# Gated linear attention and two MoE layers on one core: attention rebuilt around VectorE block transposes, alternating row halves, block-diagonal states and merged scans

## The chip, the core and the metric

The kernel runs on one core of a Trainium2 chip. The metric is the device time of one execution in microseconds, taken as the median of several runs. TensorE (PE) multiplies matrices, VectorE (DVE), ScalarE (ACT) and GpSimd (POOL) work on elements, SyncE (SP) issues most of the transfers. Each engine takes its instructions in the order in which the program lists them and waits on semaphores for the others.

## What is computed

Three steps follow one another: a gated linear attention over 4 batches, 8 heads, 768 tokens and a head width of 48, a gated MoE layer, and a mixture of four domain experts.

```python
for t in range(S):                      # attention, per batch and head
    state = alpha[:, :, t, :, None] * state + np.einsum('bhd,bhe->bhde', k[:, :, t], v[:, :, t])
    y[:, :, t] = np.einsum('bhd,bhde->bhe', q[:, :, t], state)
...
gate = 1.0 / (1.0 + np.exp(-(x @ w_gate)))        # x: 3072 x 384, d_ff 1536
x = gate * (x @ w_val) @ w_out
...
p = domain_probs / (domain_probs.sum(-1, keepdims=True) + 1e-09)
for e in range(E):                                # 4 experts of width 1024
    out += p[:, e:e + 1] * (np.maximum(x @ w1[e], 0.0) @ w2[e])
```

## The kernel before

The tokens of the attention are cut into 24 chunks of 128 (NCH; six of them, CPB, make a batch). Each chunk holds 8 heads, kept as 4 pairs (NP): one head of a pair on partitions 0 to 63 and one on 64 to 127, each 48 wide with 16 columns of padding. A chunk goes through three stages.

- Stage 1 brings alpha, k and q of a chunk, loaded token by token, into the layout with the head's width on the partitions: `s1_pe` calls `s1_t` for each, four TensorE transposes against the identity (L188), into banks 7, 6 and 5. On VectorE `s1_b` runs four scans (L203) backwards over the chunk's decays and gets the decay from each token to the chunk's end, with three small operations (L205 to L207) for the whole chunk's; `s1_k` multiplies k with it. `s1_a` runs four scans forwards (L217) for the inverse, `s1_q` multiplies q with that. `s1_range` lets ScalarE sum both for a range check, and `st_decay` decays the running state.
- Stage 2, `s2_pe`, transposes the scaled k (L233) and computes the scores, eight products of 64 rows: the four pairs of the lower half, then the four of the upper. `s2_ev` copies the transposed k out on ScalarE (L241) and masks the scores on VectorE (L244) into `pt`.
- Stage 3, `s3_pe`, multiplies transposed k with v for the state's increment, v with the masked scores, and, except in the first chunk of a batch, the old state with q. The two products for a pair of heads stand together in the order:

```python
for j in (0, 1):
    mm(X0[64 * j:64 * j + 64, p, :], vn[i][:, 2 * p + j, :], pt[j][:, p, :], True, first)
for j in (0, 1):
    r = slice(64 * j, 64 * j + 64)
    if not first:
        mm(X0[64 * j:64 * j + D, p, :], St[r, p, :], qt[i][r, p, :], False, True)
```

`s3_y` copies the result out and moves the fourth pair's part into the padding of the other three by six small transfers (L268), `s3_state` adds the increment to the state, and `s4`, two steps later, splits the result into a high and a low part as the input `xs` of the first MoE.

All fp32 products of the attention show as two matmul records each in the trace. The MoE products are three fp32r products of 512 or 384 columns each (`mm3`, all on L112).

The order of every engine is the program's own (the whole body stands under a manual schedule). A prologue takes chunks 0 to 4 through the three stages, overlapped by one chunk. The first MoE follows in six blocks of 512 tokens (bi), each in 12 steps (f). A step computes gate and value products (`gv`, 18 matmuls on banks 0 and 1), the sigmoid on ScalarE (L339), the product on VectorE (L343), its high part on ScalarE (L344) and its low part (`g_lo`: GpSimd in the first block, VectorE, L349, later), and the output products of the step before (`l2`, 9 matmuls). Into each step one stage of one chunk is woven: chunk 5 takes the first three steps, chunk 8 ends the first block, chunks 9 to 23 lie in the later ones. In the first block each step also decodes two to four units of weights that come as float64 bits: three VectorE operations a unit (L161 to L163), two on ScalarE (L155, L174), one on GpSimd, and up to four transfers on SP (L140 to L147) into four landing buffers that are refilled as they come free. Of alpha, k, q and v two chunks are held; `load` brings the next but one as soon as the transposes of a chunk have read their buffer. The second MoE follows, and takes more than half of the time; the change does not touch it.

Of the kernel before, what the change touches and what calls it, by code (L numbers as in the profile page):

```python
# [15 lines left out]
P = 128  # L16
# the scaled form holds while a chunk's running decays and their inverses stay below BOUND
# [5 lines left out]
def kernel(ctx: ExitStack, tc: tile.TileContext, q, k, v, alpha,  # L23
# [27 lines left out]
    RR = const.tile([P, 35840], F32R, tag="RR", name="RR")  # L51
    FA = const.tile([P, 9216], F32, tag="FA", name="FA")
# [3 lines left out]
    low = const.tile([P, 1], F32, tag="low", name="low")  # L56
    St = const.tile([P, NP, D], F32, tag="St", name="St")
    aend = const.tile([P, NCH * NP], F32, tag="aend", name="aend")
    pn = const.tile([P, NTT, E], F32, tag="pn", name="pn")
    psm = const.tile([P, NTT], F32, tag="psm", name="psm")  # L60
    fl = const.tile([P, (NP + 2) * NCH], F32, tag="fl", name="fl")
# [15 lines left out]
    # phase A, attention  # L77
# [21 lines left out]
    sg = [carve(LD, LT + (2 + i) * TB, TB) for i in (0, 1)]  # L99
    stg = [carve(LD, i * TB, TB) for i in range(4)]  # L100
    # phase B
# [18 lines left out]
    def load(g, part, eng=nc.sync):  # L120
        if g >= NCH:
            return
        b, c = divmod(g, CPB)
        i = g % 2
        for t, x in (((vn, v),) if part else ((an, alpha), (kn, k), (qn, q))):
            eng.dma_start(out=t[i][:, :, 0:D],
                          in_=x[b, :, c * P:(c + 1) * P, :].rearrange("h p d -> p h d"))

    # weights of MoE1 come as float64 bits: word 0 low, word 1 high
# [60 lines left out]
    def s1_pe(g, bk):  # L190
        for X, t in ((bk[2], an), (bk[1], kn), (bk[0], qn)):
            s1_t(g, X, t)
        load(g + 2, 0)

    def ends(t, g):
        return t[:, g * NP:(g + 1) * NP]

    # decay from a token to the chunk's end, and the whole chunk's
    def s1_b(g, bk):
        Bc, X0 = Ac[g % 2], pairs(bk)[2]  # L200
        lows = low.to_broadcast([P, P - 1])
        for p in range(NP):
            nc.vector.tensor_tensor_scan(Bc[:, p, 0:P - 1][:, ::-1], X0[:, p, 1:P][:, ::-1], lows, 1.0, ALU.mult, ALU.max)  # L203
        ae = ends(aend, g)
        nc.vector.tensor_tensor(ae.rearrange("p (a b) -> p a b", b=1), X0[:, :, 0:1], Bc[:, :, 0:1], ALU.mult)  # L205
        nc.vector.tensor_scalar(ae, ae, low, None, ALU.max)
        nc.vector.reciprocal(ends(fl, g), ae)  # L207

    def s1_k(g, bk):
        i = g % 2  # L210
        nc.vector.tensor_tensor(kt[i], pairs(bk)[1], Ac[i], ALU.mult)

    # its inverse, running forwards
    def s1_a(g, bk):
        X0 = pairs(bk)[2]
        for p in range(NP):
            nc.vector.tensor_tensor_scan(kb[g % 2][:, p, :], X0[:, p, :], low.to_broadcast([P, P]),  # L217
                                         ends(fl, g)[:, p:p + 1], ALU.mult, ALU.max)

    def s1_q(g, bk):  # L220
        i = g % 2
        nc.vector.tensor_tensor(qt[i], pairs(bk)[0], kb[i], ALU.mult)

    def s1_range(g, o):
        n = NP * NCH + 2 * g
        for j, t in enumerate((kb, Ac)):
            nc.scalar.activation(o, t[g % 2].rearrange("p a b -> p (a b)"), AF.Copy, accum_out=fl[:, n + j:n + j + 1])

    def s2_pe(g, bk):
        i = g % 2  # L230
        X = pairs(bk)
        for p in range(NP):
            nc.tensor.transpose(X[2][:, p, :], kt[i][:, p, :], ident)  # L233
        for j in (0, 1):
            r = slice(64 * j, 64 * j + 64)
            for p in range(NP):
                mm(X[j][:, p, :], kt[i][r, p, :], qt[i][r, p, :], True, True)

    def s2_ev(g, bk):
        X = pairs(bk)  # L240
        nc.scalar.activation(kb[g % 2], X[2], AF.Copy)  # L241
        mb = mask.rearrange("p (a t) -> p a t", a=1).to_broadcast([P, NP, P])
        for j in (0, 1):
            nc.vector.tensor_tensor(pt[j].bitcast(I32), X[j].bitcast(I32), mb, ALU.bitwise_and)  # L244

    def s3_pe(g, bk):
        i = g % 2
        first = g % CPB == 0
        X0, X1 = pairs(bk)[0:2]
        if g % CPB != CPB - 1:  # L250
            for p in range(NP):
                for j in (0, 1):
                    mm(X1[64 * j:64 * j + 64, p, 0:D], kb[i][:, p, 64 * j:64 * j + 64], vn[i][:, 2 * p + j, 0:D], True, True)
# [16 lines left out]

    def s3_state(g, bk):
        X1 = pairs(bk)[1]
        if g % CPB == 0:
            nc.vector.tensor_copy(St, X1[:, :, 0:D])
        elif g % CPB != CPB - 1:
# [465 lines left out]
```

## Time and profile before

| | |
|---|---|
| median of 3 runs | 1455.66 us (1455.57 to 1458.17) |
| span of the profiled execution | 1454.4 us |
| PE busy | 1428.7 us, 98% of the span |
| DVE busy | 686.9 us, 47% |
| ACT, POOL busy | 348.1 us, 162.9 us |
| end of the first block, from which the chain of waits is TensorE's | about 160 us |

The page is of one execution; its span lies 1.3 us below the median of the runs. A busy PE is not one at its peak, since matmuls are pipelined; what a change is worth is read from the chain of waits, stage by stage.

### The profile page before, as it was taken

How to read it: one execution, taken by the hardware profiler on the slowest of the kernel's cores; microseconds unless marked ns; L12 is line 12 of the kernel's file. 1: busy time of each engine (PE TensorE's matmuls, PEld its weight loads, DVE VectorE, ACT ScalarE, POOL GpSimd, SP SyncE). 2: the span in 40 equal slices, each digit the busy share in tenths (PEclk: the TensorE clock that was granted, in tenths of full speed). 3: DMA queues.
4: the chain of work that ended last, by engine and by line, in shares of the span. 5: the costliest groups of instructions: out<-in, count | busy, mean ns of one | idle time of the engine just before them, and what ended most of it. 6: DMA issues, size and time to landing. Idle time of an engine off the chain costs nothing.

```text
span 1454.4 us, 19314 instructions
## 1 busy us (share of the span) xinstructions
PE 1428.7 (98%) x7792; PEld 1226.1 (84%) x7792; DVE 686.9 (47%) x1235; ACT 348.1 (24%) x670; POOL 162.9 (11%) x167
## 2 busy tenths in 40 slices
PE   9889999999999999999999999999999999999998
PEld 7667787878788787879999999999999999999997
DVE  7788653434343442224444444444444444444444
ACT  3444332322222222332211111111111121111110
POOL 0344300000000000241101110110011011101000
PEclk9899999999999999999999999999999999999999
DMA  9775321312221200231000000000000000000003
GB/s 132 148 159 135 81 53 30 62 27 43 46 47 24 53 2 9 88 94 52 23 1 23 22 11 12 22 23 1 23 22 23 0 23 22 0 1 0 1 23 110
DMA packets 138640, 60.76 MB, mean 42 GB/s; under 512 B 108336, under 2 KB 133168, under 8 KB 138544
## 3 DMA queue, kind: packets, MB, share of 16 engines
q1 hardware_dynamic: 129184, 57.68, 17.1%
q10 hardware_dynamic: 9360, 1.77, 0.8%
q8 instruction: 63, 1.03, 0.3%
q14 instruction: 33, 0.27, 0.1%
HBM read 49.59 MB, written 8.65 MB: 40 GB/s over the span
## 4 chain that ended last, share of the span: by engine, by line
PE 90%; DVE 4%; DMA 3%; SPq 1%; issue 1%; ACT 0%; POOL 0%; DVEq 0%; ACTq 0%; POOLq 0%
PE bank L112 88%; PE bank L188 2%; DMA LD<-in_moe_w_gate_dram 1%; DVE LD L163 1%; DVE LD L162 1%; DMA FA<-in_q_dram 1%; DMA LD<-in_moe_w_out_dram 1%; PE bank L233 1%; SPq L268 1%; DVE LD L161 0%; DVE FA L203 0%; DVE FA L244 0%; DMA LD<-LD 0%; DVE FA L217 0%; SPq L140 0%
## 5 line engine op out<-in xcount | busy, mean ns | idle before, releaser
L112 PE MATMUL bank<-RR 128*128 128x512 f32 (+1 forms) x5976 | 1266.3, 372 | 6.4 <-ACT LD L339 2.7
L112 PEld LDWEIGHTS bank<-RR 128*128 128x128 f32 x5976 | 1092.8, 189 | 162.2 <-issue 4.2
L386 DVE SCALAR_TENSOR_TENSOR RR<-bank,RR 128x512 fp32r<-128x512 f32 x192 | 132.8, 692 | 330.9 <-ACT RR L385 330.9
L385 ACT ACTIVATE RR<-bank 128x512 fp32r<-128x512 f32 x192 | 114.9, 599 | 647.1 <-PE bank L112 647.1
L402 DVE SCALAR_TENSOR_TENSOR FA<-bank,pn,FA 128x384 f32<-128x384 f32 x360 | 221.4, 615 | 99.9 <-PE bank L112 99.9
L343 DVE TENSOR_TENSOR LD<-bank,LD 128x512 f32<-128x512 f32 x72 | 49.8, 691 | 222.4 <-PE bank L112 205.1
L369 POOL TENSOR_TENSOR RR<-LD,RR 128x384 fp32r<-128x384 f32 x64 | 63.5, 1025 | 651.3 <-PE bank L112 609.6
L112 PE MATMUL bank<-FA 64*128 64x128 f32 (+2 forms) x1088 | 95.5, 277 | 1.2 <-ACT FA L241 1.0
L112 PEld LDWEIGHTS bank<-FA 128*64 128x64 f32 (+1 forms) x1088 | 69.7, 161 | 25.0 <-issue 21.0
L339 ACT ACTIVATE LD<-bank 128x512 f32<-128x512 f32 x72 | 42.6, 592 | 174.3 <-PE bank L112 174.3
L344 ACT ACTIVATE RR<-LD 128x512 fp32r<-128x512 f32 x72 | 45.4, 631 | 140.3 <-DVE LD L343 140.3
L289 POOL TENSOR_TENSOR RR<-LD,RR 128x384 fp32r<-128x384 f32 x24 | 24.3, 1012 | 428.8 <-ACT RR L288 422.3
L203 DVE TENSOR_TENSOR_SCAN FA<-bank,low 128x127 f32<-128x127 f32 x96 | 32.5, 400 | 33.1 <-PE bank L188 33.1
L349 DVE TENSOR_TENSOR RR<-LD,RR 128x512 fp32r<-128x512 f32 x60 | 41.3, 689 | 13.4 <-ACT RR L344 13.4
L180 POOL TENSOR_TENSOR RR<-LD,RR 128x384 fp32r<-128x384 f32 x36 | 38.5, 1070 | 40.0 <-ACT RR L174 40.0
L188 PE MATMUL bank<-ident,FA 128*128 128x128 f32 x288 | 39.4, 285 | 1.7 <-ACT LD L264 1.0
L188 PEld LDWEIGHTS bank<-ident,FA 128*128 128x128 f32 x288 | 34.0, 146 | 6.3 <-ACT LD L264 1.5
L217 DVE TENSOR_TENSOR_SCAN FA<-bank,fl,low 128x128 f32<-128x128 f32 x96 | 38.4, 461 | 0.0
L163 DVE SCALAR_TENSOR_TENSOR LD<-LD 128x384 int32<-128x384 int32 x36 | 37.1, 1032 | 1.2
L244 DVE TENSOR_TENSOR FA<-bank,mask 128x512 int32<-128x512 int32 x48 | 30.9, 684 | 12.4 <-PE bank L112 12.4
L112 PE MATMUL bank<-FA,St 64*48 64x128 f32 x320 | 33.8, 288 | 0.0
L174 ACT ACTIVATE RR<-LD 128x384 fp32r<-128x384 f32 x36 | 18.8, 523 | 40.3 <-DVE LD L163 40.3
(55 smaller groups left out, 357.0 us busy)
## 6 DMA issues: line engine op xcount, KB each, us to landing
LD<-in_moe_w_dram SPq DMA_DIRECT2D x32, 384.0 KB, 3.0
FA<-in_v_dram SPq DMA_DIRECT2D x24, 192.0 KB, 2.8
LD<-in_moe_w_out_dram SPq DMA_DIRECT2D x12, 384.0 KB, 3.9
out_dram<-FA SPq DMA_DIRECT2D x24, 192.0 KB, 1.9
FA<-in_alpha_dram SPq DMA_DIRECT2D x21, 192.0 KB, 3.2
FA<-in_k_dram SPq DMA_DIRECT2D x21, 192.0 KB, 3.9
FA<-in_q_dram SPq DMA_DIRECT2D x21, 192.0 KB, 4.1
x2d<-LD SPq DMA_DIRECT2D x15, 256.0 KB, 2.3
```

Of the source, the lines that this page charges most:

```text
L112: nc.tensor.matmul(o, lhsT=l, rhs=r, start=start, stop=stop)
L163: nc.vector.scalar_tensor_tensor(wi, lw, 29, wi, ALU.logical_shift_right, ALU.bitwise_or)
L180: nc.gpsimd.tensor_tensor(unit(u, 1), wft[u % 3], unit(u, 0).bitcast(F32), ALU.subtract)
L188: nc.tensor.transpose(X[:, p * P:(p + 1) * P], t[g % 2][:, 2 * p:2 * p + 2, :].rearrange("p a b -> p (a b)"), ident)
L339: nc.scalar.activation(sg[f % 2], bank[0], AF.Sigmoid)
L343: nc.vector.tensor_tensor(s, bank[1], s, ALU.mult)
L344: nc.scalar.activation(gs[f % 2][0], s, AF.Copy)
L349: eng.tensor_tensor(gl, sg[f % 2], gh.bitcast(F32), ALU.subtract)
L369: nc.gpsimd.tensor_tensor(lo, l[:, cs], h.bitcast(F32), ALU.subtract)
L385: nc.scalar.activation(h, bk, AF.Relu)
L386: nc.vector.scalar_tensor_tensor(l, bk, 0.0, h.bitcast(F32), ALU.max, ALU.subtract)
L402: nc.vector.scalar_tensor_tensor(acc[:, tt, :], bk, pn[:, tt, e:e + 1], acc[:, tt, :], ALU.mult, ALU.add)
```

## The change

- Chunks 0 to 8 (`g < NPE`) keep the TensorE transposes, but ScalarE copies the transposed alpha into an SBUF row `Ar` before the scan reads it (`s1_al`).
- From chunk 9 on `load` brings alpha, k and q by 12 transfers of 32 partitions, four consecutive tokens to a piece, every piece into two quadrants with an offset of 32 columns; a 32x32 block transpose on VectorE (`tr32`) then takes the place of each tensor's four TensorE transposes. These chunks are loaded one chunk ahead, in one set of buffers.
- The four scans of a direction become one over 4 x 129 columns, with a column in front of each pair that resets it (`s1_b`, `s1_a`); the small operations become a memset and a reciprocal. `Bc` and `Iv` have one buffer instead of two.
- The scores alternate between the halves, on 48 rows instead of 64.
- The state `St` becomes a block-diagonal 128 x 128 matrix per pair. Its product with q comes first in stage 3, with all 128 rows and 64 columns. `s3_state` and `st_decay` work on each half apart.
- The load of the next chunks moves from the start of stage 1 to its end.

```diff
+    NPE = 9
+    BL = 32
+    TQ = P // BL
+    RB = BL + NP * TQ * D
+    ab, kbl, qb = [carve(FA, RB * i, RB) for i in range(3)]
...
+        for t, x in ((ab, alpha), (kbl, k), (qb, q)):
+            for j in (0, 1):
+                for h in (0, 1):
+                    r = BL * (2 * j + h)
+                    o = BL * (1 - h)
+                    eng.dma_start(out=t[r:r + BL, o:o + NP * TQ * D].rearrange("t (a e) -> t a e", a=NP),
+                                  in_=x[b, j:H:2, ts, :].rearrange("a (t c) d -> t a (c d)", c=TQ))
+
+    def tr32(out, t):
+        nc.vector.transpose(out.rearrange("p a (t c) -> p a c t", c=TQ),
+                            t[:, BL:].rearrange("p (a d) -> p a d", d=D)[:, :, 0:BL])
...
+    def s1_al(g, bk):
+        if g < NPE:
+            s1_t(g, bk[2], an)
+            nc.scalar.activation(At, pairs(bk)[2], AF.Copy)
+        else:
+            tr32(At, ab)
...
+    def s1_b(g):
+        nc.vector.memset(Cs[:, :, 0:1], 1.0)
+        nc.vector.tensor_tensor_scan(flat(Bc)[:, ::-1], Ar[:, 1:1 + NP * PW][:, ::-1], flat(Cs), 1.0, ALU.mult, ALU.max)
+        nc.vector.reciprocal(Cs[:, :, 0:1], Bc[:, :, 0:1])
...
+    def s1_a(g):
+        nc.vector.tensor_tensor_scan(flat(Iv), Ar[:, 0:NP * PW], flat(Cs), 1.0, ALU.mult, ALU.max)
+
+    def s1_mul(g, t, o, w, bk):
+        if g < NPE:
+            src = pairs(bk)[0]
+        else:
+            src = o[g % 2]
+            tr32(src, t)
+        nc.vector.tensor_tensor(o[g % 2], src, w[:, :, 1:PW], ALU.mult)
...
-        for j in (0, 1):
-            r = slice(64 * j, 64 * j + 64)
-            for p in range(NP):
+        for p in range(NP):
+            for j in (0, 1):
+                r = slice(64 * j, 64 * j + D)
                 mm(X[j][:, p, :], kt[i][r, p, :], qt[i][r, p, :], True, True)
...
+        def y(p, j, l, r, start):
+            nc.tensor.matmul(X0[64 * j:64 * j + 64, p, :], lhsT=l, rhs=r, start=start and p == 0, stop=True,
+                             skip_group_check=True)
+
+        if not first:
+            for p in range(NP):
+                for j in (0, 1):
+                    y(p, j, St[:, p, 64 * j:64 * j + 64], qt[i][:, p, :], True)
...
-                mm(X0[64 * j:64 * j + 64, p, :], vn[i][:, 2 * p + j, :], pt[j][:, p, :], True, first)
-            for j in (0, 1):
-                r = slice(64 * j, 64 * j + 64)
-                if not first:
-                    mm(X0[64 * j:64 * j + D, p, :], St[r, p, :], qt[i][r, p, :], False, True)
+                y(p, j, vn[i][:, 2 * p + j, :], pt[j][:, p, :], first)
...
                 if t == 1:
-                    s1_pe(g, setA)
-                    s1_b(g, setA)
+                    s1_al(g, setA)
+                    if g < NPE:
+                        s1_t(g, tk, kn)
+                        s1_t(g, tq, qn)
+                    s1_b(g)
                     s1_k(g, setA)
...
+                    if g + 2 < NPE:
+                        load(g + 2, 0)
+                    elif g + 1 >= NPE:
+                        load(g + 1, 0)
```

How the orders move. TensorE in the second block of the first MoE, one chunk from stage 1 to the end of stage 3; banks 63 and 64 hold gate and value, 65 to 67 the output, 68 to 70 are the attention's. Before:

```order
L188 MATMUL bank_68<-ident,FA 128x128 x4
L112 MATMUL bank_63<-RR 128x512 x9
L112 MATMUL bank_64<-RR 128x512 x9
L112 MATMUL bank_65<-RR 128x512 x3
L112 MATMUL bank_66<-RR 128x512 x3
L112 MATMUL bank_67<-RR 128x512 x3
L112 MATMUL bank_63<-RR 128x512 x9
L112 MATMUL bank_64<-RR 128x512 x9
L233 MATMUL bank_70<-ident,FA 128x128 x4
L112 MATMUL bank_68<-FA 128x128 x4
L112 MATMUL bank_69<-FA 128x128 x4
```

After, the same place, from the long matmuls of the step to the scores:

```order
L124 MATMUL bank_63<-RR 128x512 x9
L124 MATMUL bank_64<-RR 128x512 x9
L262 MATMUL bank_70<-ident,FA 128x128 x4
L124 MATMUL bank_68<-FA 128x128
L124 MATMUL bank_69<-FA 128x128
L124 MATMUL bank_68<-FA 128x128
L124 MATMUL bank_69<-FA 128x128
L124 MATMUL bank_68<-FA 128x128
L124 MATMUL bank_69<-FA 128x128
L124 MATMUL bank_68<-FA 128x128
L124 MATMUL bank_69<-FA 128x128
```

The 12 transposes of stage 1 are gone from this chunk, and the scores' eight products change bank, and with it the half, at every row. Stage 3 of the same chunk, before:

```order
L112 MATMUL bank_69<-FA 64x48 x8
L112 MATMUL bank_68<-FA 64x128 x2
L112 MATMUL bank_68<-FA,St 48x128 x2
L112 MATMUL bank_68<-FA 64x128 x2
L112 MATMUL bank_68<-FA,St 48x128 x2
L112 MATMUL bank_68<-FA 64x128 x2
L112 MATMUL bank_68<-FA,St 48x128 x2
L112 MATMUL bank_68<-FA 64x128 x2
L112 MATMUL bank_68<-FA,St 48x128 x2
L112 MATMUL bank_65<-RR 128x512 x3
```

And after:

```order
L124 MATMUL bank_63<-RR 128x512 x9
L124 MATMUL bank_64<-RR 128x512 x9
L282 MATMUL bank_68<-FA,St 64x128 x8
L124 MATMUL bank_69<-FA 64x48 x8
L282 MATMUL bank_68<-FA 64x128 x8
L124 MATMUL bank_65<-RR 128x512 x3
```

The state's products no longer alternate with the others and stand ahead of them. VectorE in stage 1 of such a chunk, before (L343 is the gate's product, L349 its low part):

```order
L203 SCALAR_TENSOR_TENSOR FA<-bank_70,low 128x127 x4
L205 TENSOR_TENSOR aend<-bank_70,FA 128x4
L206 TENSOR_SCALAR aend<-aend,low 128x4
L207 RECIPROCAL fl<-aend 128x4
L211 TENSOR_TENSOR FA<-bank_69,FA 128x512
L343 TENSOR_TENSOR LD<-bank_64,LD 128x512
L217 SCALAR_TENSOR_TENSOR FA<-bank_70,fl,low 128x128 x4
L222 TENSOR_TENSOR FA<-bank_68,FA 128x512
L281 TENSOR_TENSOR St<-St,aend 128x192
L349 TENSOR_TENSOR RR<-LD,RR 128x512
```

And after (the gate's product is L385, its low part L391):

```order
L154 STREAM_TRANSPOSE FA<-FA 128x4x4x32
L231 MEMSET LD 128x4
L232 SCALAR_TENSOR_TENSOR FA<-FA,LD 128x516
L233 RECIPROCAL LD<-FA 128x4
L154 STREAM_TRANSPOSE FA<-FA 128x4x4x32
L245 TENSOR_TENSOR FA<-FA 128x512
L385 TENSOR_TENSOR LD<-bank_64,LD 128x512
L237 SCALAR_TENSOR_TENSOR FA<-FA,LD 128x516
L154 STREAM_TRANSPOSE FA<-FA 128x4x4x32
L245 TENSOR_TENSOR FA<-FA 128x512
L323 TENSOR_TENSOR St<-St,FA 48x4x48 x2
L391 TENSOR_TENSOR RR<-LD,RR 128x512
```

Two block transposes come ahead of the gate's product and one behind it; none of the rows reads a bank except the gate's. ScalarE at the start of the first block, where L183 and L202 are the decode and L381 the sigmoid, after:

```order
L183 ACTIVATE LD<-LD 128x384
L202 ACTIVATE RR<-LD 128x384
L225 ACTIVATE FA<-bank_70 128x4x128
L381 ACTIVATE LD<-bank_63 128x512
L386 ACTIVATE RR<-LD 128x512
```

The copy L225 is new; it stands behind the decode and ahead of the sigmoid.

## Rows read from the trace of the kernel before

**Rows 1.** The page, parts 1 and 2: busy time by engine; granted clock in slices.

```profile
PE 1428.7 (98%) x7792; PEld 1226.1 (84%) x7792; DVE 686.9 (47%) x1235; ACT 348.1 (24%) x670; POOL 162.9 (11%) x167
...
PEclk9899999999999999999999999999999999999999
```

**Rows 2.** Chain of waits, 150 to 260 us: start, length, what, how many.

```profile
160.45 16.29 PE bank L112 x100
...
203.67 10.24 PE bank L112 x45
...
214.35 13.62 PE bank L112 x100
227.98 1.31 PE bank L188 x12
```

**Rows 3.** Timeline of TensorE, 365.5 to 377 us: start, length, engine, line, what.

```profile
365.65 1.71 PE L112 MATMUL bank<-FA 64*128 64x128 f32 x16
367.29 6.42 PE L112 MATMUL bank<-RR 128*128 128x512 f32 x27
373.63 0.91 PE L112 MATMUL bank<-FA 128*64 128x48 f32 x20
374.47 0.42 PE L112 MATMUL bank<-FA,St 64*48 64x128 f32 x4
374.82 0.44 PE L112 MATMUL bank<-FA 128*64 128x128 f32 x4
...
376.99 0.50 PE L112 MATMUL bank<-RR 128*128 128x512 f32 x1
```

**Rows 4.** Timeline of TensorE, third stages that end and begin a batch.

```profile
247.89 0.44 PE L112 MATMUL bank<-FA 128*64 128x128 f32 x4
...
250.77 2.35 PE L112 MATMUL bank<-RR 128*128 128x512 f32 x9
...
273.03 1.56 PE L112 MATMUL bank<-FA 128*64 128x48 f32 x32
274.52 2.34 PE L112 MATMUL bank<-RR 128*128 128x512 f32 x9
```

**Rows 5.** TensorE in equal windows: length, busy (instructions), clock, DMA share, GB/s.

```profile
365.75:366.19 0.44, 0.44 (x4) 1.00 0.00 0
366.19:366.63 0.44, 0.44 (x9) 1.00 0.00 0
```

**Rows 6.** Groups by line, one form each: busy us, mean ns, idle before.

```profile
L343 DVE TENSOR_TENSOR LD<-bank,LD 128x512 f32<-128x512 f32 x72 | 49.8, 691 | 222.4 <-PE bank L112 205.1 <-ACT LD L339 17.3
...
L203 DVE TENSOR_TENSOR_SCAN FA<-bank,low 128x127 f32<-128x127 f32 x96 | 32.5, 400 | 33.1 <-PE bank L188 33.1
...
L281 DVE TENSOR_TENSOR St<-St,aend 128x192 f32<-128x192 f32 x20 | 7.0, 350 | 0.1
```

**Rows 7.** Timelines of VectorE and ScalarE around 150 us.

```profile
149.37 1.25 DVE L163 SCALAR_TENSOR_TENSOR LD<-LD 128x384 int32<-128x384 int32 x1
150.54 1.34 DVE L203 TENSOR_TENSOR_SCAN FA<-bank,low 128x127 f32<-128x127 f32 x4
...
153.05 0.68 DVE L343 TENSOR_TENSOR LD<-bank,LD 128x512 f32<-128x512 f32 x1
...
150.65 0.53 ACT L174 ACTIVATE RR<-LD 128x384 fp32r<-128x384 f32 x1 [1.17 <-DVE LD L163]
```

**Rows 8.** Timeline of the prologue, ScalarE's fourth y and its transfers.

```profile
40.73 0.58 ACT L264 ACTIVATE LD<-bank 128x512 f32<-128x512 f32 x1
...
44.15 3.68 SPq L268 DMA_DIRECT2D LD<-LD  x6
```

**Rows 9.** Timeline of SP's queue at 92 us.

```profile
92.53 2.07 SPq L126 DMA_DIRECT2D FA<-in_q_dram  x1
```

**Rows 10.** Timeline of VectorE in a first stage, 225 to 234 us.

```profile
226.02 0.68 DVE L349 TENSOR_TENSOR RR<-LD,RR 128x512 fp32r<-128x512 f32 x1
...
233.51 0.69 DVE L343 TENSOR_TENSOR LD<-bank,LD 128x512 f32<-128x512 f32 x1 [2.45 <-PE bank L112]
```

More of the change, by code (lines that the diff above doesn't have):

```diff
@@ L51 @@
     RR = const.tile([P, 35840], F32R, tag="RR", name="RR")
-    FA = const.tile([P, 9216], F32, tag="FA", name="FA")
+    FA = const.tile([P, 9240], F32, tag="FA", name="FA")
     LD = const.tile([P, 6912], F32, tag="LD", name="LD")
@@ L124, in load @@
         i = g % 2
-        for t, x in (((vn, v),) if part else ((an, alpha), (kn, k), (qn, q))):
-            eng.dma_start(out=t[i][:, :, 0:D],
-                          in_=x[b, :, c * P:(c + 1) * P, :].rearrange("h p d -> p h d"))
+        ts = slice(c * P, (c + 1) * P)
+        if part:
+            eng.dma_start(out=vn[i][:, :, 0:D], in_=v[b, :, ts, :].rearrange("h p d -> p h d"))
+            return
+        if g < NPE:
+            for t, x in ((an, alpha), (kn, k), (qn, q)):
+                eng.dma_start(out=t[i][:, :, 0:D], in_=x[b, :, ts, :].rearrange("h p d -> p h d"))
+            return
+        for t, x in ((ab, alpha), (kbl, k), (qb, q)):
[8 more added lines that the diff above has]
+                            t[:, BL:].rearrange("p (a d) -> p a d", d=D)[:, :, 0:BL])
     def load_w(u):
@@ L188, in s1_t @@
             nc.tensor.transpose(X[:, p * P:(p + 1) * P], t[g % 2][:, 2 * p:2 * p + 2, :].rearrange("p a b -> p (a b)"), ident)
[L190 to L201, printed above, removed]
-        for p in range(NP):
[L203 to L207, printed above, removed]
@@ L209, in s1_k, with flat @@
-    def s1_k(g, bk):
[L210 to L218, printed above, removed]
+    def flat(t):
+        return t.rearrange("p a b -> p (a b)")
+    def s1_al(g, bk):
[4 more added lines that the diff above has]
+            tr32(At, ab)
@@ L220, in s1_q @@
+    def s1_k(g, bk):
+        s1_mul(g, kbl, kt, Bc, bk[1:])
     def s1_q(g, bk):
-        i = g % 2
-        nc.vector.tensor_tensor(qt[i], pairs(bk)[0], kb[i], ALU.mult)
+        s1_mul(g, qb, qt, Iv, bk)
     def s1_range(g, o):
-        n = NP * NCH + 2 * g
-        for j, t in enumerate((kb, Ac)):
-            nc.scalar.activation(o, t[g % 2].rearrange("p a b -> p (a b)"), AF.Copy, accum_out=fl[:, n + j:n + j + 1])
+        for j, t in enumerate((Iv, Bc)):
+            nc.scalar.activation(o.rearrange("p (a b) -> p a b", a=NP), t[:, :, 0:P], AF.Copy,
+                                 accum_out=fl[:, 2 * g + j:2 * g + j + 1])
@@ L269, in s3_y, with diag @@
                                   in_=y[64 * j + sp * c:64 * j + sp * (c + 1), NPM, :])
+    def diag(j):
+        return St[64 * j:64 * j + D, :, 64 * j:64 * j + D]
     def s3_state(g, bk):
         X1 = pairs(bk)[1]
[L273 to L276 removed]
+        for j in (0, 1):
+            x = X1[64 * j:64 * j + D, :, 0:D]
+            if g % CPB == 0:
+                nc.vector.tensor_copy(diag(j), x)
+            elif g % CPB != CPB - 1:
+                nc.vector.tensor_tensor(diag(j), x, diag(j), ALU.add)
     def st_decay(g):
         if g % CPB:
[L280 to L281 removed]
+            for j in (0, 1):
+                ae = Bc[64 * j:64 * j + D, :, 0:1].to_broadcast([D, NP, D])
+                nc.vector.tensor_tensor(diag(j), diag(j), ae, ALU.mult)
     def s4(g):
@@ L529 @@
                 nc.gpsimd.memset(t[i][:, :, D:HW], val)
-        nc.vector.memset(low, 1.0 / BOUND)
         nc.vector.memset(one, 1.0)
-        for i in (0, 1):
-            nc.vector.memset(Ac[i][:, :, P - 1:P], 1.0)
+        nc.vector.memset(Cs, 1.0 / BOUND)
+        nc.vector.memset(Ar, 0.0)
+        nc.gpsimd.memset(St, 0.0)
         nc.scalar.activation(flt, one, AF.Sigmoid)
```

48 lines of the change are left out of this document (26 added, 22 removed).

## The prediction

> **What bounds the kernel now.** I read the page's busy line first: TensorE is busy 98% of the 1454.4 us span, VectorE 47%, and the granted clock is at its upper level (2.4 GHz) in nearly every slice [rows 1]. A busy share alone does not say that TensorE is the limit, so the second view is the chain of waits. From 160.45 us on it is a chain of TensorE pieces with nothing between them [rows 2]: per attention chunk 12 input transposes (1.31 us), 45 long matmuls (10.24 us, so 0.228 us each), 4 transposes of kt (214.35 - 203.67 - 10.24 = 0.44 us), and a piece of 13.62 us that holds the scores, the long matmuls around them and the whole third stage. In that stretch every microsecond taken off TensorE is a microsecond off the end, unless another engine comes late instead. Before 160 us it is different: VectorE decoding weights, the SP queue and DMA alternate on the chain, and TensorE savings there count for nothing. Chunk 8's second and third stage and all of chunks 9 to 23 lie behind that point. So the sum is made over 16 score stages, 16 third stages and 15 first stages; the profiled execution's span lies 1.3 us under the median of 1455.66 us, and I take the savings off the median.
>
> **Input transposes (chunks 9 to 23).** The 12 matmuls of a first stage go; VectorE transposes 32x32 blocks in their place. The chain prices them at 1.31 us per chunk [rows 2], and each was 0.109 us of TensorE time. 15 x 1.31 = 19.7 us. No reason lets this be a loss on TensorE itself.
>
> **Scores.** Eight fp32 products are 16 matmul records of 64 rows. Before, all of the lower half come first, then all of the upper; from the first of them to the next long matmul it takes 367.29 - 365.65 = 1.64 us [rows 3]. After, the halves alternate. Do two halves run at once? The windows say that they do where the queue happens to offer both: 0.44 us in the middle of the stage hold 9 records where the 0.44 us before hold 4 [rows 5]. Eight records of one half at the even pace (0.44 us for 4, 0.11 us each) and a drain of some 0.2 us is 1.09 us, if the other half hides under them. I take 1.64 - 1.09 = 0.55 us; the ends are 0 (no overlap beyond today's) and 0.82 (half of 1.64, as if nothing overlapped today). 16 x 0.55 = 8.8 us.
> By the Trainium skill ("TensorE: Matmul & The Clock Gate", Part 3, The mechanism) matmuls start and end strictly in program order; then the first half could not overlap with the second in today's order, and the change would gain the 0.82. The jump from 4 to 9 records in equal windows speaks against that, but matmul ends in a trace are modelled.
>
> **State products.** Before, in a usual chunk each pair of pt products (128 rows x 64 columns) alternates with a pair of state products (64 x 48). Each group of four records takes 374.82 - 374.47, about 0.35 us, although four records that share the array two and two would need 0.22. The whole stage runs 376.99 - 373.63 = 3.36 us [rows 3]. A chunk that starts a batch has no state products: its kb and pt products stream through in 274.52 - 273.03 = 1.49 us [rows 4]. The change gives the state products the same 128 x 64 shape and puts all eight ahead of the others, so its stage is that stream plus eight pairs at 0.11 us: 1.49 + 0.89 = 2.38. The saving is 0.98 us in 11 chunks. In the three chunks that end a batch (no kb products) it was 250.77 - 247.89 = 2.88 [rows 4]; 1.49 less eight pairs of 48 columns (0.50) plus 0.89 is 1.88, saving 1.0. Chunks 12 and 18 start batches and save nothing. 11 x 0.98 + 3 x 1.0 = 13.8 us. The ends: 0, if the drains stay, and 13.8.
>
> **VectorE in the first stage.** This is the new cover that must hold. A chunk's first stage loses eight scans and three small operations and gets three block transposes (T each), two scans of 516 columns, a memset and a reciprocal; the state's two updates become four. The trace has no transpose on VectorE. Plain operations give 350 ns for 192 columns and 691 for 512, so 1.07 ns a column on 145 ns; a scan of 127 columns in 400 ns is then 2.0 ns a column, and 516 columns are 1.18 us [rows 6]. T is bounded below by the 512-column operation, 0.69 us, and above by the scan's pace, 145 + 512 x 2.0 = 1.17 us; I take 0.7, as no arithmetic is repeated in it. By the skill's page "VectorE: DVE Perf Modes" (The three transpose paths) a 128x128 bf16 tile takes 311 ns; four of them would be an estimate of 1.24 us for T, with the same sum.
> Is there room? VectorE gets past the previous step's last operation at 226.02 + 0.68 = 226.7, 227.1 with the longer state update [rows 10], and no longer waits for transposes. kt is ready at 227.1 + 2T + 2.1 (memset, scan, reciprocal, product), the gate product follows the matmuls, and qt, decay and the gate's low part end at about 233.1 + 3T even if T pushes the gate product. The second long block that needs that low part comes 45 long matmuls, 4 transposes and the scores (10.24 + 0.44 + 1.1) after the point where the 12 transposes stood, 227.98 [rows 2]: at 239.8. So TensorE starts to wait only from T = 2.2 us; before the change VectorE stood idle 2.45 us in that place [rows 10]. I cost it at nothing.
>
> **Loads.** Each chunk from 9 on comes by 12 transfers instead of 3, in 768-byte pieces instead of 192, and each piece twice. SP issues them a step and more ahead, within a chunk of 23 us; what is queued behind them there (v, the y moves) is used two steps later. Cost nothing.
>
> **The first 160 us.** Chunks 0 to 8 keep TensorE transposes and get a ScalarE copy of alpha ahead of the scan. ScalarE works in order, so the scan now waits for what is queued before the copy. In the first block the scan followed the decode directly (149.37 + 1.25, scan at 150.54) and the gate product came at 153.05 [rows 7]. Now: the rest of the decode's ScalarE step to 151.18, copy 0.58, scan and small operations 1.5, kt 0.66: about 153.85, +0.8. The second scan gives back 0.4, the two extra state operations cost 0.7: +1.1 for four chunks, +4.4. In the prologue three copies of 0.58 with about 0.5 of queue each make the fourth y 3.2 us later; it was ready at 41.31 and its moves were issued only at 44.15 [rows 8], so 2.8 of that is covered: +0.4. Against this the loads move behind the step's weight load, and chunk 9's leave a decode step: SP spent 2.07 us on one q load [rows 9], with a weight load as the next row of its queue; twice that is -4. Sum about +1. Ends: nothing covered, 9 copies at 1.2 plus 4 x 0.7 = +13.6; or only the gain, -4.
>
> **Sum.** 19.7 + 8.8 + 13.8 = 42.3 saved, 1 lost: 1455.66 - 41.3 = 1414.4 us.
>
> **Rivals.**
> (a) The copies queue for longer than I think and nothing covers them: +13.6 instead of +1, 1427 us. For it: VectorE and SP are on the chain there. Against: DMA waits of the same stretch hide part. 13%.
> (b) Alternating halves don't overlap, because a switch between halves costs what a switch of shape costs: 1423. Against: [rows 5]. 7%.
> (c) Scores gain the full 0.82, the rule of the Trainium skill above: 16 x 0.27 less, 1410. 6%.
> (d) The state products still drain, so the change doesn't do there what it says: 1428. For it: nothing in the trace has that accumulate order. 3%.
> (e) Slower: block transposes on VectorE become the bound of a first stage. They write with a stride, and the trace has no such row. Beyond T = 2.2 each microsecond of T costs 3 us in 15 chunks; the gain of 41.3 us (2.75 a chunk) is gone at T = 2.2 + 0.92 = 3.1 us, 4.5 times the 512-column row; at T = 3.5 the time is 1414.4 + 15 x 3.9 = 1473. 5%, of which 4 beyond 3.1 us or close to it.
> The forecast itself keeps 66%.
>
> **How the numbers follow.** The forecast's own spread is about +-6 us, mostly the first 160 us (the chain's piece right behind them, [rows 2], took 16.29 us where the same piece later took 13.62). With (c) below and (a), (b), (d) above, the range is 1405 to 1428. It leaves out (e) and the tails of the others. Two kernels this long are told apart at 0.2%, 3 us: faster 0.95, same 0.01, slower 0.04.
>
> **What would show it.** The chain after 160 us should have no transpose piece of 1.31 us from chunk 9 on; scores should take about 1.1 us from first record to the next long matmul, a usual third stage 2.4. A chunk's period should fall from 25.6 to about 22.8 us, with TensorE without idle time. Block transposes should be 0.7 to 1.2 us on VectorE. The first block should end within some microseconds of 160. I am wrong if TensorE waits for VectorE in the first or second stages of chunks 9 to 23, if the scores keep 1.6 us, or if the first block ends past 170.

## The result, and the profile after

| | before | after |
|---|---|---|
| median of the runs | 1455.73 us (1455.57 to 1458.17) | 1421.07 us (1420.57 to 1421.63) |
| ratio, 95% interval | | 0.9757 [0.9743, 0.9771] |
| span of the profiled execution | 1454.4 us | 1418.9 us |

The change is faster by 34.7 us, 2.4%; the forecast was 41.3 us. The time lies inside the range and 6.7 us above the forecast. The page of after, parts 1 and 2, answers to [rows 1]:

```profile
PE 1375.0 (97%) x7612; PEld 1196.4 (84%) x7612; DVE 741.7 (52%) x1151; ACT 353.6 (25%) x679; POOL 165.8 (12%) x171
...
PEclk9898999999999999999999999999999999999999
```

TensorE has lost 180 records (15 chunks of 12 transposes) and 53.7 us of busy time, VectorE has gained 54.8 us. The chain of waits of after, 165 to 260 us (start, length, what, how many), answers to [rows 2]:

```profile
176.21 1.88 PE bank L124 x7
...
200.80 1.02 PE bank L282 x16
201.82 0.45 PE bank L124 x16
202.27 0.89 PE bank L282 x16
203.16 12.47 PE bank L124 x54
215.63 0.44 PE bank L262 x4
216.06 7.44 PE bank L124 x43
223.50 1.02 PE bank L282 x16
```

It is TensorE's alone from 176.21 us on (before from 160.45), and the piece of 12 transposes is gone. From one third stage to the next it takes 223.50 - 200.80 = 22.70 us. The timeline of TensorE in a later chunk of after, 335 to 354 us, answers to [rows 3]:

```profile
335.63 1.09 PE L282 MATMUL bank<-FA,St 128*64 128x128 f32 x16
336.55 0.62 PE L124 MATMUL bank<-FA 128*64 128x48 f32 x16
337.00 1.06 PE L282 MATMUL bank<-FA 128*64 128x128 f32 x16
337.99 12.54 PE L124 MATMUL bank<-RR 128*128 128x512 f32 x54
...
350.89 1.16 PE L124 MATMUL bank<-FA 48*128 48x128 f32 x16
351.99 2.34 PE L124 MATMUL bank<-RR 128*128 128x512 f32 x9
```

The third stage takes 337.99 - 335.63 = 2.36 us instead of 3.36, the scores 351.99 - 350.89 = 1.10 instead of 1.64. The groups by line of VectorE (busy us, mean ns, idle before) answer to [rows 6]:

```profile
L154 DVE STREAM_TRANSPOSE FA<-FA 128x512 f32<-128x512 f32 x45 | 48.7, 1083 | 0.1
L232 DVE TENSOR_TENSOR_SCAN FA<-FA,LD 128x516 f32<-128x516 f32 x24 | 31.3, 1302 | 17.8 <-ACT FA L225 17.1
L237 DVE TENSOR_TENSOR_SCAN FA<-FA,LD 128x516 f32<-128x516 f32 x24 | 29.3, 1221 | 0.0
```

A block transpose takes 1.08 us. The first scan waited 17.1 us in all for the copy L225 on ScalarE, all of it in chunks 0 to 8. That VectorE is still no bound later is seen in its timeline at the gate product of such a chunk's first stage, where it idles until TensorE delivers, as in [rows 10]:

```profile
344.51 0.69 DVE L385 TENSOR_TENSOR LD<-bank,LD 128x512 f32<-128x512 f32 x1 [1.52 <-PE bank L124]
```

The gain does not begin at 160 us. Here is the first record behind chunk 8's third stage, on TensorE's timeline, of before:

```profile
174.37 2.37 PE L112 MATMUL bank<-RR 128*128 128x512 f32 x9
```

and of after:

```profile
180.38 2.79 PE L124 MATMUL bank<-RR 128*128 128x512 f32 x11
```

After is 6.0 us late at this point. From here to the end before takes 1454.4 - 174.37 = 1280.0 us and after 1418.9 - 180.38 = 1238.5: 41.5 us saved.

### The profile page after: what moved, and what is told of

The parts are those of the page before. It is cut to its first block, busy times and chain, and to the rows that moved or that the text cites. A ratio compares the mean times of both kernels' runs of the same rounds, so it can differ in the third digit from the quotient of the medians.

```text
span 1418.9 us, 19045 instructions
## 1 busy us (share of the span) xinstructions
PE 1375.0 (97%) x7612; PEld 1196.4 (84%) x7612; DVE 741.7 (52%) x1151; ACT 353.6 (25%) x679; POOL 165.8 (12%) x171
## 3 DMA queue, kind: packets, MB, share of 16 engines
q10 hardware_dynamic: 9360, 1.77, 0.9%
## 4 chain that ended last, share of the span: by engine, by line
PE 87%; DVE 6%; DMA 3%; ACT 1%; issue 1%; SPq 1%; POOL 0%; DVEq 0%; ACTq 0%; POOLq 0%
PE bank L124 84%; PE bank L282 2%; DVE LD L191 1%; DVE LD L190 1%; DVE LD L189 1%; DVE FA L232 1%; DVE FA L273 1%; DMA LD<-in_moe_w_gate_dram 1%; DMA LD<-in_moe_w_out_dram 1%; DMA LD<-LD 1%; DMA FA<-in_alpha_dram 1%; PE bank L262 1%; DMA LD<-in_moe_w_val_dram 1%; DMA FA<-in_k_dram 0%; DVE FA L237 0%
## 5 line engine op out<-in xcount | busy, mean ns | idle before, releaser
L385 DVE TENSOR_TENSOR LD<-bank,LD 128x512 f32<-128x512 f32 x72 | 49.7, 691 | 175.3 <-PE bank L124 158.7
L381 ACT ACTIVATE LD<-bank 128x512 f32<-128x512 f32 x72 | 42.8, 594 | 147.6 <-PE bank L124 147.6
L391 DVE TENSOR_TENSOR RR<-LD,RR 128x512 fp32r<-128x512 f32 x60 | 47.9, 798 | 13.4 <-ACT RR L386 12.6
L154 DVE STREAM_TRANSPOSE FA<-FA 128x512 f32<-128x512 f32 x45 | 48.7, 1083 | 0.1
L124 PE MATMUL bank<-FA 48*128 48x128 f32 (+1 forms) x704 | 42.4, 262 | 0.3 <-DVE FA L245 0.3
L124 PEld LDWEIGHTS bank<-FA 48*128 48x128 f32 (+1 forms) x704 | 36.7, 170 | 5.9 <-issue 4.9
L232 DVE TENSOR_TENSOR_SCAN FA<-FA,LD 128x516 f32<-128x516 f32 x24 | 31.3, 1302 | 17.8 <-ACT FA L225 17.1
L282 PE MATMUL bank<-FA 128*64 128x128 f32 x384 | 28.5, 282 | 6.3 <-DVE FA L273 6.2
L202 ACT ACTIVATE RR<-LD 128x384 fp32r<-128x384 f32 x36 | 18.9, 524 | 45.4 <-DVE LD L191 41.7
L237 DVE TENSOR_TENSOR_SCAN FA<-FA,LD 128x516 f32<-128x516 f32 x24 | 29.3, 1221 | 0.0
L282 PEld LDWEIGHTS bank<-FA 128*64 128x64 f32 x384 | 22.7, 141 | 7.8 <-DVE FA L273 6.5
```

The costliest lines, as they stand in the source:

```text
L124: nc.tensor.matmul(o, lhsT=l, rhs=r, start=start, stop=stop)
L154: nc.vector.transpose(out.rearrange("p a (t c) -> p a c t", c=TQ), t[:, BL:].rearrange("p (a d) -> p a d", d=D)[:, :, 0:BL])
L232: nc.vector.tensor_tensor_scan(flat(Bc)[:, ::-1], Ar[:, 1:1 + NP * PW][:, ::-1], flat(Cs), 1.0, ALU.mult, ALU.max)
L282: nc.tensor.matmul(X0[64 * j:64 * j + 64, p, :], lhsT=l, rhs=r, start=start and p == 0, stop=True, skip_group_check=True)
L385: nc.vector.tensor_tensor(s, bank[1], s, ALU.mult)
L391: eng.tensor_tensor(gl, sg[f % 2], gh.bitcast(F32), ALU.subtract)
```

## Experiments

Each edit is made in after. The kernels ran in groups, each on one chip; the difference named is to a kernel of the same group, the ratio to the kernel before on the same chip.

**Three changes undone, one at a time.** First after itself, as the measure of its group.

> The changed kernel once more, on the chip of the next three runs, as their base. Every theory expects 1421 us within 1.5 us, with a first block that ends about 9 us later than before the change and a chunk period of 22.7 us behind it.

It took 1421.85 us, ratio 0.9755 [0.9739, 0.9772].

Scores in the old order:

```diff
-        for p in range(NP):
-            for j in (0, 1):
+        for j in (0, 1):
+            for p in range(NP):
                 r = slice(64 * j, 64 * j + D)
                 mm(X[j][:, p, :], kt[i][r, p, :], qt[i][r, p, :], True, True)
```

> The changed kernel with the eight score products in the old order, the lower half's four and then the upper's. If alternating lets the two row halves run side by side, as I forecast, the score stage goes back from 1.1 to 1.64 us and 16 chunks behind the first block cost 16 x 0.55 = 8.8 us more: about 1430. If nothing overlapped in the old order, as matmuls strictly in program order would have it, it is 16 x 0.82: about 1434. If the order of the halves does not matter: 1421.

1430.72 us, ratio 0.9816 [0.9800, 0.9833]: 8.9 us slower than after. The timeline of TensorE in this kernel shows the scores and what follows them:

```profile
357.38 1.71 PE L124 MATMUL bank<-FA 48*128 48x128 f32 x16
359.01 6.20 PE L124 MATMUL bank<-RR 128*128 128x512 f32 x26
```

The stage is 1.63 us long again, although it has 48 rows as in after: the order makes the difference, not the rows. This decides rivals (b) and (c). By the Trainium skill ("TensorE: Matmul & The Clock Gate", Part 3, The mechanism) matmuls start and end strictly in program order; 16 x 0.82 = 13.1 us would then have been lost here. The measured 8.9 us does not agree with that and fits 16 x 0.55. The starts of the records in the trace of before do not agree either: the first record of the upper half starts at 366.20 us, and three of the lower half's eight start behind it, the last at 366.53, though all of them stand ahead of it in the program. So TensorE does not start its products strictly in the order in which the program lists them.

State products in the old order and shape:

```diff
-        if not first:
-            for p in range(NP):
-                for j in (0, 1):
-                    y(p, j, St[:, p, 64 * j:64 * j + 64], qt[i][:, p, :], True)
...
-                y(p, j, vn[i][:, 2 * p + j, :], pt[j][:, p, :], first)
+                mm(X0[64 * j:64 * j + 64, p, :], vn[i][:, 2 * p + j, :], pt[j][:, p, :], True, first)
+            for j in (0, 1):
+                if not first:
+                    r = slice(64 * j, 64 * j + D)
+                    mm(X0[64 * j:64 * j + D, p, :], St[r, p, 64 * j:64 * j + D], qt[i][r, p, :], False, True)
```

> The changed kernel with the state products back as 64 x 48 pieces, alternating pair by pair with the others (the block-diagonal state is kept, only its diagonal blocks are read). If each switch of shape drains the array, as I forecast, a usual third stage goes back from 2.4 to 3.35 us and 14 chunks behind the first block cost 13.8 us more: about 1435. If the saving came from the shorter wait for the masked scores alone, TensorE being busy anyway, it stays at 1421.

1440.89 us, ratio 0.9889 [0.9872, 0.9905]: 19.0 us slower, 5 more than expected. TensorE's timeline gives a third stage of 350.44 - 347.09 = 3.35 us, 0.99 more than in after, and 14 x 0.99 = 13.9 us is what was expected:

```profile
347.09 0.91 PE L124 MATMUL bank<-FA 128*64 128x48 f32 x20
...
350.44 1.89 PE L124 MATMUL bank<-RR 128*128 128x512 f32 x7
```

The rest arises in the prologue. The windows of this kernel (length, busy time and records of PE, PEld, DVE, ACT, POOL, granted clock, DMA share, GB/s) show chunk 1's third stage:

```profile
23.08:28.58 5.50, 5.50 (x33) 2.51 (x34) 2.31 (x4) 1.45 (x4) 0.00 (x0) 0.50 0.62 132
```

At the same place after has:

```profile
23.27:25.38 2.11, 2.11 (x24) 1.94 (x25) 2.01 (x3) 0.90 (x3) 0.00 (x0) 1.00 0.33 98
```

The clock stood at its lower level (1.2 GHz) there, in after at the upper one, and VectorE's state update waited for these products:

```profile
28.56 0.74 DVE L317 TENSOR_TENSOR St<-bank,St 48x192 f32<-48x192 f32 x2 [3.09 <-PE bank L124]
```

The first sigmoid of the first block (L381) starts 4.3 us later than in after of the same group (67.04 against 62.78 us), and the last as much later. So the old order costs 14 us by its length; the other 4 to 5 us stand with a prologue at half the clock, and why the clock fell in this kernel and not in after was not tested. The run puts back the order and the 64 x 48 shape together; which of the two is worth the 0.99 us a stage it does not part.

TensorE transposes for all chunks:

```diff
-    NPE = 9
+    NPE = 24
```

> The changed kernel with all 24 chunks on the TensorE transposes and the ScalarE copy of alpha, no block transposes. If TensorE time is all that counts behind the first block, 15 chunks cost 1.31 us more each: 1421 + 19.7 = 1441. If the block transposes on VectorE hold TensorE up somewhere, less than that comes back: each microsecond of such a wait per chunk takes 15 us off, so 1426 to 1436 would show it. If instead the ScalarE copy delays the first stage also behind the first block, more: 1445 and above.

1442.37 us, ratio 0.9898 [0.9882, 0.9915]: 20.5 us slower. The chain of waits has the piece back, once a chunk, unhidden:

```profile
231.77 1.31 PE bank L216 x12
```

**Is VectorE's cover as large as reckoned?** Each block transpose is done twice or three times.

```diff
+        for _ in range(2):
-        nc.vector.transpose(out.rearrange("p a (t c) -> p a c t", c=TQ),
+            nc.vector.transpose(out.rearrange("p a (t c) -> p a c t", c=TQ),
...
```

> The changed kernel with every block transpose done twice, so that T is about 2.1 us instead of 1.08. By the prediction's room (TensorE waits only from T = 2.2 us) no change, 1421 to 1424. If the block transposes are already at the edge of the room, 15 chunks pay up to 3.2 us each: up to 1470.

1422.59 us, ratio 0.9767 [0.9752, 0.9782]. 15 x 3 more transposes, 49 us more of VectorE, cost nothing that can be measured (after stands at 0.9757 and 0.9755, and the intervals overlap). The room is used up, though: from 195 to 545 us the weight loads of the scores wait nine times for the third transpose's product (L246), 0.2 us at most, the matmuls not at all.

> The changed kernel with every block transpose done three times, T about 3.2 us. By the prediction's rival (e), each microsecond beyond 2.2 costs 3 us in each of 15 chunks: 1421 + 45 = about 1466, slower than before the change. If VectorE's room is larger than I worked out, less; at no wait 1422.

1477.63 us, ratio 1.0150 [1.0134, 1.0166]: 55 us slower than with two, and slower than before. TensorE's timeline in one chunk:

```profile
323.07 0.66 PE L263 MATMUL bank<-ident,FA 128*128 128x128 f32 x4 [0.39 <-ACT bank L256]
325.50 1.16 PE L124 MATMUL bank<-FA 48*128 48x128 f32 x16 [1.77 <-DVE FA L246]
```

and the piece behind it on the chain of waits:

```profile
325.50 9.13 PE bank L124 x43
```

TensorE now waits for what hangs on VectorE: 0.39 us ahead of the transposes of kt, for ScalarE's range check (L256, which itself waited for VectorE's scan), and 1.77 for qt (L246 is the product of the third transpose). The same 43 records take 7.47 us with two transposes, 1.66 less. In those 1.66 us TensorE waits for nothing: behind the wait for qt the granted clock falls to its lower level, as a window shows (length, busy, clock, DMA share, GB/s):

```profile
327.60:329.80 2.20, 2.20 (x6) 0.50 0.05 15
```

That makes 3.8 us in this chunk, but not in all. In the 14 chunks from 195 to 545 us TensorE waits 27.1 us in all for L246 and 4.1 for L256, and the piece takes 9.1 us in nine of them and 7.5 in five; 9 x 1.6 = 14.4 us, so some 46 us together of the 55. So TensorE begins to wait between T = 2.2 and 3.3 us, as reckoned, and at 3.3 the whole gain is gone and more, as rival (e) has it beyond 3.1. What waits are the scores, for qt, not the long block that needs the low part, and the price is higher than the expected 45 us because the clock falls as well.

**What keeps the first block late?** Four kernels, in one group. The scans of chunks 0 to 8 read the bank again, pair by pair, without the copy (the second scan alike):

```diff
             s1_t(g, bk[2], an)
-            nc.scalar.activation(At, pairs(bk)[2], AF.Copy)
...
+        if g < NPE:
+            X0 = pairs(setA)[2]
+            for p in range(NP):
+                nc.vector.tensor_tensor_scan(Bc[:, p, 0:P][:, ::-1], X0[:, p, :][:, ::-1], low.to_broadcast([P, P]),
+                                             1.0, ALU.mult, ALU.max)
+        else:
...
```

> The changed kernel, but chunks 0 to 8 scan alpha from its bank again, four scans a direction, and the ScalarE copy is gone; everything from chunk 9 on is as changed. If the first block is late because VectorE's scan waits for ScalarE's queue and the copy, the gate's product in a first stage comes 1.3 us sooner, of which the longer second scan takes 0.4 back: 0.9 x 3 chunks, about 2 for the chunk that opens the block and 1.8 in the prologue, 6 to 7 us in all: 1415 to 1416. If the doubled state operations or the loads make it late, 1421 to 1422.

The copy made by VectorE:

```diff
-            nc.scalar.activation(At, pairs(bk)[2], AF.Copy)
+            nc.vector.tensor_copy(At, pairs(bk)[2])
```

> The changed kernel with the copy of alpha on VectorE instead of ScalarE: 0.6 us more work for VectorE in each of 9 chunks, no wait for ScalarE's queue. If the wait is what costs, some 0.5 us a chunk comes back in the first block and up to 3 us at its start and in the prologue: about 1417. If VectorE's own work is what costs, it gets slower by up to 9 x 0.6: 1422 to 1427.

The loads of the chunks up to 8 back at the start of stage 1:

```diff
                         s1_t(g, tq, qn)
+                        if g + 2 < NPE:
+                            load(g + 2, 0)
...
-                    if g + 2 < NPE:
-                        load(g + 2, 0)
-                    elif g + 1 >= NPE:
+                    if g + 1 >= NPE:
```

> The changed kernel with the loads of chunks 7 and 8 back at the start of the first stage, ahead of the step's weight loads in SP's queue. My prediction put 2 us on each load that the change moves behind the weight loads: 4 us slower, 1426. If the first block hangs on VectorE's own decoding and not on the loads, as its trace after the change suggests, no change: 1421 to 1423.

One half of the state update and of the decay left out:

```diff
-        for j in (0, 1):
+        for j in (0,):
             x = X1[
...
-            for j in (0, 1):
+            for j in (0,):
                 ae = Bc[
```

> The changed kernel with the state's increment and decay done for the lower half alone (the upper half's part of the state is left out and stays zero), so that VectorE has as many state operations as before the change. If those two extra operations of 0.35 us are on VectorE's chain in the first block and the prologue, 0.7 us for each of four chunks and for some of the prologue's: 2.8 to 5 us less, 1417 to 1419. If they hide in VectorE's waits: 1421 to 1422.

| kernel | median, us | ratio to before | sigmoid of step 0, 3, 6, 9, 11 of the first block, later than in before, us |
|---|---|---|---|
| after | 1421.07 | 0.9757 [0.9743, 0.9771] | 2.2, 4.9, 6.2, 8.1, 8.9 |
| loads at the start | 1421.87 | 0.9766 [0.9753, 0.9779] | 3.4, 6.1, 7.4, 9.3, 10.1 |
| half a state | 1418.70 | 0.9743 [0.9729, 0.9756] | 2.1, 4.1, 4.8, 5.4, 5.6 |
| copy on VectorE | 1416.87 | 0.9731 [0.9718, 0.9744] | 0.3, 0.5, 1.8, 3.6, 4.8 |
| scans from the bank | 1414.11 | 0.9714 [0.9701, 0.9727] | -0.1, 0.4, 0.6, 1.5, 1.7 |

The last column is the start of the sigmoid in each profiled execution less its start in before (59.6, 89.1, 119.9, 151.1 and 169.1 us). The first number of a row scatters from one execution to the next: in five kernels whose prologue is that of after, the sigmoid of step 0 starts between 61.8 and 63.0 us, and after is at the low end. From step 0 to step 11 after and the loads at the start lose the same 6.7 us. Against the loads at the start, 1421.87 us in the same group: the place of the loads of chunks 7 and 8 is worth nothing (chunk 9's, which the change moves too, stay where the change put them), the second half of the state's operations 3 us, ScalarE's part of the copy 5 us, copy and merged scan together 8 us. The costs do not add up to what after is late (3 + 8 is more than 8.9). The chain of waits of the kernel with the scans on the bank has waits for weights in that stretch (2.00 us from 129.96, 2.60 from 135.32), so a step that VectorE no longer delays probably waits for its weights instead; no run tested that.

Where the copy costs is seen in two places. In the prologue, VectorE's timeline of after:

```profile
19.85 1.23 DVE L232 TENSOR_TENSOR_SCAN FA<-FA,LD 128x516 f32<-128x516 f32 x1 [1.91 <-ACT FA L225]
...
28.84 1.23 DVE L232 TENSOR_TENSOR_SCAN FA<-FA,LD 128x516 f32<-128x516 f32 x1 [2.15 <-ACT FA L225]
```

and of the kernel whose scans read the bank:

```profile
17.87 1.37 DVE L235 TENSOR_TENSOR_SCAN FA<-bank,low 128x128 f32<-128x128 f32 x4
...
25.09 1.37 DVE L235 TENSOR_TENSOR_SCAN FA<-bank,low 128x128 f32<-128x128 f32 x4
```

A chunk takes 28.84 - 19.85 = 9.0 us instead of 25.09 - 17.87 = 7.2, because the copy stands behind the y copy (L299) on ScalarE, and both behind the loads that ScalarE issues in the prologue (L143, 25.27 to 27.68 us here). The last of these, of q, refills the buffer that the TensorE transposes of q read, and so comes after them. The chain of waits of after shows it, from those transposes (L216) to the scan:

```profile
26.91 0.60 PE bank L216 x4
27.51 0.17 ACTq L143
...
27.72 0.12 ACT LD L299
...
28.22 0.60 ACT FA L225
...
28.84 1.24 DVE FA L232
```

So VectorE waits for the loads, the y copy and its own copy. TensorE, which waits with it, falls to the lower clock; a window of after, and then the same window of before:

```profile
33.60:36.60 3.00, 3.00 (x17) 2.67 (x18) 1.92 (x6) 1.37 (x5) 0.00 (x0) 0.56 0.55 134
```

```profile
33.60:36.60 3.00, 2.31 (x28) 1.94 (x27) 2.90 (x9) 1.80 (x4) 0.00 (x0) 1.00 0.73 136
```

17 records where before does 28. The fourth y and its transfers, in the timelines of ScalarE and SP of after, answer to [rows 8]:

```profile
45.29 0.58 ACT L299 ACTIVATE LD<-bank 128x512 f32<-128x512 f32 x1
...
45.95 3.68 SPq L303 DMA_DIRECT2D LD<-LD  x6
```

The y is 4.6 us late, its transfers 1.8. In the first block, the timelines of ScalarE, GpSimd and VectorE of after at one first stage, which answer to [rows 7]:

```profile
93.46 0.58 ACT L225 ACTIVATE FA<-bank 128x512 f32<-128x512 f32 x1
...
93.63 1.01 POOL L208 TENSOR_TENSOR RR<-LD,RR 128x384 fp32r<-128x384 f32 x1 [1.05 <-ACT RR L202]
...
94.07 1.67 DVE L232 TENSOR_TENSOR_SCAN FA<-FA,LD 128x516 f32<-128x516 f32 x1 [1.06 <-ACT FA L225]
...
96.44 0.68 DVE L385 TENSOR_TENSOR LD<-bank,LD 128x512 f32<-128x512 f32 x1
```

VectorE waits 1.06 us for the copy, and then the scan takes 1.67 us where it took 1.23 in the prologue: it starts while GpSimd's decode operation (93.63 to 94.64) runs. With the scans on the bank, VectorE and GpSimd in such a stage:

```profile
120.15 1.37 DVE L235 TENSOR_TENSOR_SCAN FA<-bank,low 128x128 f32<-128x128 f32 x4
...
120.75 1.01 POOL L209 TENSOR_TENSOR RR<-LD,RR 128x384 fp32r<-128x384 f32 x1 [1.05 <-ACT RR L203]
```

These take 1.37 us beside GpSimd and without it (17.87 above). So the merged scan, 0.14 us faster than four in the prologue, is 0.3 us slower in the first block, and the copy comes on top.

**Two more.** Block transposes from chunk 6 on:

```diff
-    NPE = 9
+    NPE = 6
...
-                        load(NPRO + 2, 0)
```

> The changed kernel with block transposes from chunk 6 instead of chunk 9, so also for three chunks of the first block. TensorE loses 3 x 1.31 us there. If the first block hangs on VectorE, its three more transposes (3.2 us a chunk) less the wait for the ScalarE copy (1 us) cost about 2.2 us for three chunks: 1428. If TensorE counts there as it does later: 1418.

1427.62 us, ratio 0.9805 [0.9790, 0.9820], 5.0 us slower than the transposes done twice, in the same group: in the first block the savings of TensorE count for nothing. What costs is VectorE's extra work or the 12 transfers that take the place of three on SP, among the weight loads: seven pieces of 0.42 to 0.44 us of their issue (L150) stand on the chain of waits between 102.23 and 105.5 us. The run does not part the two. And the fastest so far, scans from the bank, with the state's decay given to GpSimd:

```diff
-                nc.vector.tensor_tensor(diag(j), diag(j), ae, ALU.mult)
+                nc.gpsimd.tensor_tensor(diag(j), diag(j), ae, ALU.mult)
```

> Scans from the bank for chunks 0 to 8 (which gave 1414.1) and both halves' state decays moved from VectorE to GpSimd. If VectorE's chain alone sets the first block, 0.7 us for each of four chunks and some of the prologue come off: 1411. If GpSimd, busy with low parts there, or a wait for it takes that back: 1414 or more.

1413.49 us, ratio 0.9705 [0.9692, 0.9719]. It is the lowest time, but its interval overlaps with that of the scans from the bank alone; a gain from GpSimd is not shown. Either of the two beats both kernels, after by 6 to 8 us.

## Why the prediction was right, and what it missed

| step | forecast, us | measured, us |
|---|---|---|
| input transposes | -19.7 | 20.5 lost when undone |
| scores | -8.8 | 8.9 lost when undone; 1.10 us a stage (1.09 forecast) |
| state products | -13.8 | stage of 2.36 (2.38 forecast); 14 x 0.99 = 13.9 |
| VectorE's new work, chunks 9 on | 0 | 0, TensorE without idle time |
| the same, from chunk 8's third stage to the end | -40.8 | -41.5 |
| up to the end of chunk 8's third stage | -0.5 (+1 less 0.55 and 0.98) | +6.0 |

- **The chain.** TensorE's bound from chunk 9 on, the period (22.70 us, forecast about 22.8) and the three savings came as worked out. That the transposes, scores and products are worth what they are long was shown by undoing each, for the products after taking off what that run lost in its prologue.
- **Block transposes.** T was taken as 0.7 us and measured 1.08, inside the bounds of 0.69 and 1.17 and near the upper one, the scan's pace; the argument for the lower end (no arithmetic is repeated) did not hold. The estimate of 1.24 worked out from the Trainium skill's page "VectorE: DVE Perf Modes" (The three transpose paths) was nearer to the measured 1.08 than the value taken. The miss cost nothing because the point where TensorE begins to wait was put at 2.2: two transposes in place of one (T about 2.2) changed nothing, three made rival (e) come true. The point held, but by another wait than the one it was worked out from, the scores' for qt and not the long block's for the low part.
- **The first 160 us, the step that failed.** It was sized at +1 and came out at 6.0 + 1.5 = +7.5, within its ends of -4 and +13.6. Three terms of it were wrong. First, the gain of 4 us for the moved loads does not show: putting those of chunks 7 and 8 back changed nothing (chunk 9's were not put back), and that SP spent 2.07 us on one load [rows 9] was no reason that the end waits for it. Second, the prologue costs 1.8 us instead of 0.4 (up to 1.2 more in other executions): the fourth y comes 4.6 us later, not 3.2, of which 2.8 are covered as forecast. The wait for the copy is 1.9 to 2.2 us, where half a microsecond of queue was reckoned with, because y's copy and the loads that ScalarE issues stand ahead of it. Third, the four chunks of the first block cost (8.9 - 1.8) / 4 = 1.8 us each instead of 1.1: from the end of the decode operation at 93.00 to the gate product at 96.44 it takes 3.44 us, against 2.5 in before [rows 7], the second scan gives back the 0.4 reckoned (1.22 us instead of 1.60), and the split state operations cost about the 0.7 reckoned (the half left out brought 3 us for four chunks). Some 0.4 us a chunk stays unaccounted for. The three add 4 + 1.4 + 2.8 = 8.2 us to the +1; 9.2 us is about the 8.9 us by which the last sigmoid is late; 1.0 of it the third stage behind it saves, and the other 1.9 are made up before 180 us, which was not followed further.
- **Rivals.** (b), (c) and (d) fell, by the scores' order and the timeline of the third stage. (a), the queueing copies, is what happened in kind, at half its price: 7.5 of 13.6 us. The prediction named ScalarE's queue as the cause and then reckoned with about one operation in it.
- **Signs foretold.** Scores, third stage, period and transposes showed as said. The first block ends past the 170 us that the text gave as a sign of being wrong (the chain is TensorE's from 176.21 us, the last sigmoid starts at 178.0 instead of 169.1). The sign pointed to the right term; the total stayed in the range because its upper end took in the whole price of rival (a).

## What to carry to other kernels

A saving on the engine that bounds a stage is worth its length there and nothing in a stage that another engine bounds; the same change gained 2.9 us a chunk in one and cost 1.8 in the other, so its parts should be switched by stage (here by leaving the scans of the early chunks on the bank, worth 6 to 8 us). A copy to make an operand fit costs its place in the other engine's queue, which is as long as everything ahead of it, the transfers which that engine issues included, and not as the copy. Give the array's two halves alternating work, and keep products of one shape together: both are gains that can be read off a timeline beforehand.

## What the runs showed of the hardware

- A 32x32 block transpose of 128x512 fp32 with a strided output takes 1.08 us, 1.6 times the 0.69 us of a plain operation of that size.
- VectorE operations that read two operands from SBUF are drawn out where they start while GpSimd works: the scan above, 1.67 instead of 1.23 us, and in the steady stretch the gate's low part, 1.40 instead of 0.69, in the timelines of VectorE and GpSimd of after:

```profile
337.97 0.69 DVE L391 TENSOR_TENSOR RR<-LD,RR 128x512 fp32r<-128x512 f32 x1
...
348.72 1.40 DVE L391 TENSOR_TENSOR RR<-LD,RR 128x512 fp32r<-128x512 f32 x1
...
348.46 1.11 POOL L331 TENSOR_TENSOR RR<-LD,RR 128x384 fp32r<-128x384 f32 x1 [21.60 <-ACT RR L330]
```

  The operation ends about as late as if it had begun when GpSimd's ended. By the Trainium skill ("SBUF — State Buffer", Who interferes with whom) a VectorE instruction with two SBUF inputs and a GpSimd instruction that reads SBUF exclude one another, and whoever comes first blocks the other. These rows agree, to 0.2 us.
- Sixteen records of 48 rows take 1.10 us where the halves alternate, 1.63 in two runs of eight, and the second run of eight starts while three records of the first have still to start; a third stage whose products change shape at every second product takes 0.99 us longer than one in which they stand together in one shape.
- With three transposes TensorE waited 1.7 to 2.4 us a chunk ahead of the scores; in nine chunks of 14 the 43 records behind took 9.1 us instead of 7.5, and in the one shown with its clock the granted clock stood at its lower level (1.2 GHz) for 2.2 us and more.
